# Two more PSUM banks for a first batch, its key load in two, and the next batch's keys ahead of a weight load

## Chip, cores, metric

One core of one Trainium2 chip. The metric is device time in microseconds (us), the median of several runs. Before: 419.73 us (3 runs, 419.38 to 420.42). The profile's span, from the first to the last instruction, is some 2 us shorter than the run that it was taken from.

## The reference

```python
# attention: 8 batches, 16 query heads, 4 key/value heads, 384 tokens, head size 64
k, v  = np.repeat(k, 4, axis=1), np.repeat(v, 4, axis=1)
attn  = softmax(q @ k.T / 8)
x     = (attn @ v) -> tokens x 1024          # 3072 x 1024
h     = np.maximum(x @ w_in, 0.0)            # w_in 1024 x 2048
out   = h * h @ w_out                        # w_out 2048 x 1024
```

The batches flow through one core: attention of batch b+1 is woven between the feed-forward matmuls of batch b. Only batch 0 has no feed-forward work beside it, so its start is the loose end of the kernel.

## The kernel before, where the change touches it

The kernel is recorded by a small scheduler in Python at build time. It keeps a table of assumed costs, and by it decides in which order each engine gets its work. On the chip each engine then runs its list in that order and waits on semaphores. A wrong assumed cost makes no wrong result, but it makes an engine wait in front of something that is not there yet.

First loads of batch 0 (keys and two pairs of query heads), on the queues of SyncE and ScalarE:

```python
keys("sync", 0, 1)          # key group 0, 96 KB
queries("scalar", 0)        # 192 KB
queries("sync", 1)          # 192 KB
keys("scalar", 1, HKV)      # key groups 1 to 3 in one load, 288 KB
```

All other loads are issued by GpSimd, in this order, with copies of keys (`dup_k`) and values (`aug_v`) between them. A copy that waits for its data holds up every load behind it:

```python
load_q(0, 4, 8)             # queries of group 1: "the first query load"
...
load_v(0); load_q(0, 8, 12, 0.6); load_q(0, 12, 16, 0.6)
dup_k(0, 1, 2)
load_w_in(0)
dup_k(0, 2, 3)
load_k(1)
dup_k(0, 3, 4)
aug_v(0, "gpsimd")
load_q(1, 0, 8); load_q(1, 8, 16)
load_w_in(1)
load_v(1)
dup_k(1)
for i in range(2, 6): load_w_in(i)
```

Which PSUM banks transposes and head pairs (the products with the values) may use while batch 0 still has scores to compute; scores have banks 0 to 3:

```python
LOW, MID, HIGH = tuple(range(6)), (4, 5), (6, 7)
...
spare = MID if first else tuple(i for i in LOW if i not in held)
```

w_in comes in eight pieces of 512 KB. Four tiles of the first feed-forward ("lanes", 32 matmuls of 128 rows) need pieces 0 and 1. The first "quad" of four tiles follows (64-row matmuls); its first 16 matmuls need the third piece, and its 17th needs the fourth.

The softmax here doesn't subtract the row's maximum and nothing guards it: scores larger than these inputs give would overflow.

## Time and profile before

| | before |
|---|---|
| time, median (range) | 419.73 us (419.38 to 420.42) |
| span of the profiled run | 418.2 us |
| TensorE busy | 413.4 us, 99% |
| first query load lands | 6.86 us |
| third exponential starts | 7.27 us |
| lanes end | 28.66 us |
| fourth piece of w_in lands | 30.66 us |

Times of landing are those at which the last of a load's 16 semaphore increments came, read from the trace. "Lanes end" is the start of the last lane matmul plus the 0.16 us from one such matmul to the next; the profile models the end of that matmul another 0.16 us later. Besides the lines that the prediction shows, two views of before are needed. The list of loads issued from 1 to 6 us (what it moves, issuing queue, KB, us from issue to landing):

```profile
q_st<-in_q_dram POOLq DMA_DIRECT2D x3, 192.0 KB, 5.5
k_f<-in_k_dram ACTq DMA_DIRECT2D x1, 288.0 KB, 4.0
```

The three key groups land 4.0 us after issue. The second view is the timeline of GpSimd (start, length, engine, line, operation; in brackets an idle time before it and what ended it):

```profile
6.67 0.52 POOL L270 CAST k_dup<-k_f 128x384 bf16<-128x384 f32 x1
7.12 0.76 POOL L209 DMA_DIRECT2D k_st<-in_k_dram  x1
...
9.10 1.76 POOL L241 DMA_DIRECT2D q_st<-in_q_dram  x2
10.84 0.89 POOL L252 DMA_DIRECT2D w_in_sb<-in_moe_w_in_dram  x1
...
13.68 1.47 POOL L270 COPY k_dup<-k_st 128x1536 bf16<-128x1536 bf16 x1 [1.20 <-DMA k_st<-in_k_dram]
```

GpSimd issues both query loads of batch 1 and the second piece of w_in before it waits for anything. Its one wait of 1.20 us, at 12.5, comes when much is under way.

### The profile page before, as it was taken

The page shows a single profiled execution, that of the slowest core. Times are in us where ns is not written, and L with a number is a line of the kernel's source. Part 1 is how long each engine was busy: PE and PEld are TensorE (multiplying, and loading weights), DVE is VectorE, ACT ScalarE, POOL GpSimd, SP SyncE. Part 2 cuts the span into 40 slices and gives each one's busy share as a digit, 9 for nine tenths or more (in the row PEclk, how much of TensorE's full clock was granted, in tenths as well). Part 3 has the DMA queues.
Part 4 walks back from the last instruction along what each step waited for, and adds up shares of the span by engine and source line. Part 5 has one row for each costly group of instructions (what it writes and reads, how often), then busy time and mean ns, then how long its engine had stood idle before and what let it go on. Part 6 is the DMA issues. An engine that isn't in the chain of part 4 may idle for free.

```text
span 418.2 us, 9601 instructions
## 1 busy us (share of the span) xinstructions
PE 413.4 (99%) x4308; PEld 236.2 (56%) x4331; DVE 198.6 (47%) x434; ACT 159.0 (38%) x181; POOL 48.0 (11%) x63
## 2 busy tenths in 40 slices
PE   9999999999999999999999999999999999999997
PEld 6666754557446574455645565456744557445544
DVE  3664751357413782156811666125841458324312
ACT  6948610495009610284104840069000870004300
POOL 8680000323030000200020000000000000000000
PEclk9999999999999999999999999999999999999999
DMA  9999999999996019900499005710052001420012
GB/s 179 190 190 200 206 188 170 260 190 120 187 186 101 2 39 201 209 7 2 61 211 183 2 2 107 183 52 2 3 125 77 27 2 20 122 79 10 0 74 78
DMA packets 96921, 44.40 MB, mean 106 GB/s; under 512 B 77296, under 2 KB 90864, under 8 KB 96880
## 3 DMA queue, kind: packets, MB, share of 16 engines
q0 software_dynamic: 36544, 17.44, 32.5%
q1 hardware_dynamic: 59664, 25.86, 27.7%
q8 instruction: 34, 0.56, 0.5%
q10 hardware_dynamic: 672, 0.49, 0.4%
q14 instruction: 7, 0.06, 0.0%
HBM read 35.65 MB, written 12.58 MB: 115 GB/s over the span
## 4 chain that ended last, share of the span: by engine, by line
PE 97%; ACT 2%; issue 0%; DVE 0%
PE ps L524 39%; PE ps L462 34%; PE ps L367 8%; PE ps L341 7%; PE ps L425 6%; ACT expT L351 2%; PE ps L588 1%; PE ps L400 0%; PE ps L298 0%; PE ps L315 0%; DVE y_sb L533 0%
## 5 line engine op out<-in xcount | busy, mean ns | idle before, releaser
L351 ACT ACTIVATE expT<-ps 128x1024 bf16<-128x1024 f32 (+1 forms) x146 | 136.0, 1022 | 133.4 <-PE ps L341 133.4
L524 PE MATMUL ps<-w_out_sb,h2T 128*128 128x512 bf16 (+2 forms) x761 | 165.7, 375 | 1.2
L462 PE MATMUL ps<-xT,w_in_sb 64*128 64x384 bf16 x1728 | 160.3, 323 | 0.0
L524 PEld LDWEIGHTS ps<-w_out_sb,h2T 128*128 128x128 bf16 x784 | 75.2, 98 | 86.6
L462 PEld LDWEIGHTS ps<-xT,w_in_sb 64*128 64x128 bf16 x1728 | 83.1, 94 | 57.8 <-DVE hr L475 2.1
L475 DVE TENSOR_SCALAR hr<-ps 128x384 f32<-128x384 f32 x108 | 55.2, 553 | 79.0 <-PE ps L462 79.0
L533 DVE COPY y_sb<-ps 128x512 f32<-128x512 f32 (+2 forms) x49 | 33.4, 681 | 112.3 <-PE ps L524 112.3
L341 PE MATMUL ps<-qT,kT 64*128 64x512 bf16 (+2 forms) x384 | 54.3, 326 | 0.3 <-ACT expT L351 0.3
L482 DVE TENSOR_TENSOR h2T<-hr 128x384 bf16<-128x384 f32 x102 | 50.0, 551 | 0.0
L367 PEld LDWEIGHTS ps<-v_aug,expT 128*128 128x128 bf16 x1152 | 37.0, 97 | 5.7 <-issue 1.1
L367 PE MATMUL ps<-v_aug,expT 128*128 128x65 bf16 x1152 | 39.1, 193 | 0.2 <-issue 0.2
L382 DVE TENSOR_TENSOR o_sb<-ps,rinv 128x384 bf16<-128x384 f32 x64 | 35.7, 558 | 2.2
L425 PE MATMUL ps<-xT,w_in_sb 128*128 128x384 bf16 x160 | 27.7, 326 | 0.0
L435 ACT ACTIVATE h2T<-hr 128x384 bf16<-128x384 f32 x20 | 10.3, 522 | 44.3 <-DVE hr L433 44.3
L341 PEld LDWEIGHTS ps<-qT,kT 64*128 64x128 bf16 x384 | 17.8, 94 | 15.6 <-issue 2.1
L275 POOL COPY v_aug<-v_st 128x768 bf16<-128x768 bf16 x8 | 6.6, 830 | 158.4 <-PE ps L367 99.5
L479 ACT ACTIVATE h2T<-hr 128x384 bf16<-128x384 f32 x6 | 3.1, 523 | 51.7 <-DVE hr L475 51.7
L425 PEld LDWEIGHTS ps<-xT,w_in_sb 128*128 128x128 bf16 x160 | 15.4, 98 | 9.7 <-DVE xT L406 0.2
L433 DVE TENSOR_SCALAR hr<-ps 128x384 f32<-128x384 f32 x20 | 11.0, 557 | 12.1 <-PE ps L425 12.1
L241 POOL DMA_DIRECT2D q_st<-in_q_dram x17 | 14.8, 883 | 0.9 <-POOLq L829 0.8
L376 DVE RECIPROCAL rinv<-ps 128x6 f32<-128x6 f32 x64 | 11.9, 186 | 4.4 <-PE ps L367 4.4
L209 POOL DMA_DIRECT2D k_st<-in_k_dram x7 | 5.3, 755 | 43.6 <-DMA qT<-q_st 43.6
(29 smaller groups left out, 65.2 us busy)
## 6 DMA issues: line engine op xcount, KB each, us to landing
out_dram<-y_sb SPq DMA_DIRECT2D x47, 256.0 KB, 2.6
q_st<-in_q_dram POOLq DMA_DIRECT2D x14, 384.0 KB, 8.2
w_in_sb<-in_moe_w_in_dram POOLq DMA_DIRECT2D x8, 512.0 KB, 14.8
w_out_sb<-in_moe_w_out_dram POOLq DMA_DIRECT2D x4, 1024.0 KB, 27.4
v_st<-in_v_dram POOLq DMA_DIRECT2D x8, 192.0 KB, 9.7
k_st<-in_k_dram POOLq DMA_DIRECT2D x7, 192.0 KB, 4.5
q_st<-in_q_dram POOLq DMA_DIRECT2D x3, 192.0 KB, 5.5
xT<-o_sb SPq DMA_TRANSPOSE x28, 2.8
```

Source lines behind the costliest of these rows:

```text
L241: i = R.add("gpsimd", lambda g: g.dma_start(q_st[st][:, h0:h1, :], q[b, h0:h1].rearrange("h (p j) d -> p h (j d)", j=NJ)), writes=[("q_st" ...
L341: mm = pe.matmul(ps[:, base + x, m * wide:(m + 1) * wide], kT[b % 2][64 * x:64 * x + 64, u, :], q_cols(b, u // NJ, x, c0, c0 + wide))
L351: R.add("scalar", lambda e: e.activation(dst, src, AF.Exp, scale=0.125), reads=keys, writes=[("expT", (b * NU + u) % NEX, t) for u, _, _ i ...
L367: m = pe.matmul(po[:, f - 6 * s2, 0:D + 1], w, v_aug[b % 2][:, g * NJ + j, 0:D + 1], start=(j == 0), stop=(j == NJ - 1))
L376: R.add("vector", lambda e: e.reciprocal(rinv[r].ap().unsqueeze(2), po[:, :, D:D + 1]), reads=[("bank", i)], writes=[("rinv", r)], cost=0.22)
L382: R.add("vector", lambda e: e.tensor_tensor(dst, srcv, rbv, ALU.mult), reads=[("bank", i), ("rinv", r)], writes=[("o_sb", o, s2)], cost=0.48)
L425: m = pe.matmul(bank(i)[:, 0:S], w_in_sb[:, kc, c * 128:(c + 1) * 128], xT[b % NXT][:, kc, :], start=(kc == 0), stop=(kc == NKC - 1))
L462: m = pe.matmul(bank(4 + xs[x])[:, 0:S], w_in_sb[r, kc, c * 128:(c + 1) * 128], xT[b % NXT][r, kc, :], start=(phase < 2 and kc == 0), stop ...
L475: R.add("vector", lambda e, r=r, i=i: e.tensor_scalar_max(hr[r][:, :], bank(4 + i)[:, 0:S], 0.0), reads=[("bank", 4 + i)], writes=[("hr", ...
L482: hr_read[r] = (R.add("vector", lambda e, c=c, r=r: e.tensor_tensor(h2T[:, c, :], hr[r][:, :], hr[r][:, :], ALU.mult), reads=[("hr", r)], ...
L524: m = pe.matmul(bank(i)[:, 0:n], h2T[:, c, i3 * 128:(i3 + 1) * 128], w_out_sb[:, c, c0:c1], start=(c == 0), stop=(c == NFC - 1))
L533: R.add("vector", lambda e: e.tensor_copy(ysl, bank(i)[:, 0:n]), reads=[("bank", i)], writes=[("y", yb)], cost=0.08 + n / 960)
```

## The change

The intent: give TensorE more useful work in batch 0. With four banks instead of two, transposes and head pairs need not wait for their copies; batch 1's keys, loaded ahead of w_in, can be transposed then; and the second key group comes in a load of its own, to be there sooner.

```diff
-        keys("scalar", 1, HKV)
+        keys("scalar", 1, 2)
+        keys("sync", 2, HKV)
@@
     dup_k(0, 1, 2)
+    load_k(1)
+    dup_k(0, 2, 3)
     load_w_in(0)
-    dup_k(0, 2, 3)
-    load_k(1)
     dup_k(0, 3, 4)
     aug_v(0, "gpsimd")
     load_q(1, 0, 8)
+    dup_k(1, 0, 2)
     load_q(1, 8, 16)
+    dup_k(1, 2, 4)
     load_w_in(1)
     load_v(1)
-    dup_k(1)
@@
-        spare = MID if first else tuple(i for i in LOW if i not in held)
+        spare = tuple(i for i in MID + HIGH if i not in held) if first else tuple(i for i in LOW if i not in held)
```

Below, the three parts are called "banks", "split" (of the key load) and "order" (of the loads).

## The prediction

> **What bounds the kernel now.** I read the page's busy shares first, then the chain that ended last in order of time, then the timeline of the first 31 us, then each load's time to landing, because the change touches only the first two batches.
>
> The page, busy shares and chain by engine:
>
> ```profile
> PE 413.4 (99%) x4308; PEld 236.2 (56%) x4331; DVE 198.6 (47%) x434; ACT 159.0 (38%) x181; POOL 48.0 (11%) x63
> ...
> PE 97%; ACT 2%; issue 0%; DVE 0%
> ```
>
> TensorE is nearly the whole chain; 2% of 418.2 us is about 8 us of ScalarE. The chain in order of time says where those 8 us lie:
>
> ```profile
> 0.77 3.04 PE ps L588 x27
> ...
> 5.79 8.08 ACT expT L351 x10
> 13.87 0.05 issue
> 13.92 0.39 PE ps L341 x4
> ...
> 24.72 0.17 PE ps L298 x3
> 24.89 0.34 PE ps L315 x6
> ...
> 28.82 0.76 PE ps L462 x8
> ```
>
> The columns are start, length, what. From 5.79 to 13.87 the ten exponentials of the first batch are the chain, and after 13.92 it is TensorE to the end. The second batch's transposes (lines 298 and 315) lie on it at 24.72: 4 x 0.17 + 2 x 0.34 = 1.36 us. So the change can gain only by putting useful TensorE work into holes before 13.9. The timeline shows the holes (start, length, engine, line):
>
> ```profile
> 6.30 0.53 PE L298 MATMUL ps<-ident,k_dup 128*128 128x128 bf16 x3
> ...
> 6.62 0.34 PE L588 MATMUL ps<-const-bfloat16-1.0 128*128 128x128 bf16 x2
> ...
> 6.89 0.34 PE L341 MATMUL ps<-qT,kT 64*128 64x384 bf16 x2
> ...
> 8.32 0.83 POOL L275 COPY v_aug<-v_st 128x768 bf16<-128x768 bf16 x1
> 8.47 0.35 PE L588 MATMUL ps<-const-bfloat16-1.0 128*128 128x128 bf16 x3
> ...
> 10.92 0.44 PE L367 MATMUL ps<-v_aug,expT 128*128 128x65 bf16 x9
> ...
> 13.32 0.34 PE L400 MATMUL ps<-ident,o_sb 128*128 128x128 bf16 x3
> ```
>
> Line 588 is filler. Holes and filler: 6.62 to 6.89 (0.27), 8.05 to 8.20 (0.15), 8.47 to 8.85 (0.38), about 0.1 before 10.25, and about 0.4 between the transposes of 13.32 and the scores of 13.92. Sum: some 1.3 us. That is the ceiling at this end.
>
> There is a second wall later. Waits of 28 to 31.5 us, and the load that ends the wait (KB, us from issue to landing):
>
> ```profile
> PEld ps L462 <- DMA w_in_sb<-in_moe_w_in_dram: 0.4, 1, 0.4
> ```
>
> ```profile
> w_in_sb<-in_moe_w_in_dram POOLq DMA_DIRECT2D x1, 512.0 KB, 14.7
> ```
>
> That load is the fourth piece of w_in, issued at 15.97: it lands at 30.67, and the timeline has TensorE start on it at 30.71. So at 30.7 the kernel is already loading-bound, for a moment.
>
> **What the Trainium skill says.** "PSUM — Partial Sum Buffer", the four PSUM rules: one matmul output goes to one of 8 banks; "Perfetto Trace Analysis", Optimizing Tensor Performance, says independent groups should rotate through banks so that evacuation overlaps the next matmuls. Here batch 0 had banks 4 and 5 for this, each held for the transpose plus a VectorE copy of 0.36 to 0.56 us; the filler at 6.62 agrees, since keys' and queries' copies still held both banks. "DMA: Bandwidth & Descriptors", Issuing engines are not separate DMA queues: loads from different engines run on the same 16 DMA engines, so another issuer saves issue time only. The trace agrees that the engines are the limit (the page has busy tenths of 9 in the first twelve slices of its DMA row). "TensorEngine Tiling (Array Packing)", Key Properties: a change of tiling mode drains TensorE. Each score group (64-row tiles) shows it: about 0.1 us lost on entering and again on leaving, so 0.2 us around each group is not a hole that banks can fill.
>
> **Part by part.**
> *Keys in two loads.* It takes 288 KB as 96 + 192 KB. Before, the load of 1.23 landed after 4.0 us, at 5.23. But GpSimd issues queries until 5.24 and starts the copy of group 1 at 5.33, so an earlier landing brings at most 0.1 us. Off the path: zero.
>
> *Second batch's keys ahead of w_in.* In landing order the loads are last queries of batch 0 (9.9), w_in piece 0 (5.78 + 6.8 = 12.6), k1 (7.12 + 6.5 = 13.6), first queries of batch 1 (9.10 + 7.7 = 16.8). k1 took 13.6 - 12.6 = 1.0 us of the stream, so k1 comes at about 10.9 and w_in piece 0 at about 13.6; all later loads keep their place. The first matmul on w_in is at 15.40, so the 1.0 us later landing still precedes it. The GpSimd copy of 1.47 us, at 13.68 before, becomes two of 0.75 us at about 10.9 and 12.5. It now holds up the issue of the loads behind it by some 2 us, but those have a backlog (second half of batch 1's queries: landing at 18.8, issue about 11.7), so no landing moves.
>
> *Two more banks.* These open until the feed-forward lanes take banks 6 and 7 at about 15. The queue order is fixed at build time from a table of costs in the kernel, which I use for order alone. By hand I get: query transposes of group 1 before the third score group instead of after it; the first value product near 9 instead of 10.92; keys group 0 of batch 1 near 13; queries group 0 of batch 1 near 15.5; keys group 1 near 18. So 0.17 + 0.34 + 0.17 = 0.68 us of the 1.36 leave the chain at 24.7, and products and output transposes move up a little.
>
> Costs, because TensorE executes in order:
> 1. The query transposes that now stand at 6.62 need the load issued at 1.23, which took 5.6 us: 6.86. They run 6.9 to 7.24, and the third score group moves from 6.89 to about 7.34. Third exponential: from 7.27 to about 7.7. Cost to the exponential chain 0.44 us.
> 2. The first value product stands ahead of the sixth score group and needs the value copy (8.32 + 0.83 = 9.15). It delays that group to about 9.66, the exponential to 10.03 instead of 9.38: chain late by 0.65 to 0.7.
> 3. The queries of batch 1 land at 16.8; TensorE would reach their transposes at about 16.1: a wait of some 0.7 us that was not there, with no other work behind it that may overtake.
>
> The lanes' end: in queue order about 0.5 us less work lies ahead of it (0.68 off the end, little else, minus the work displaced). Against this stand about 0.5 us of lag from steps 1 and 2 and 0.7 from step 3: 0.7 later than 28.75, i.e. near 29.5. The following 1.3 us of feed-forward and two score groups then carry it past 30.7, so the wait of 0.15 us for w_in (in excess of the matmul before it) vanishes: net about +0.55. Without step 3 the lanes end where they did: 0. After that TensorE is bound by its own work with fixed order, and a shift is carried to the end undiminished.
>
> **Rivals.**
> (a) *The gain arrives.* If none of the three waits occurs, the lanes end 0.5 to 1.0 us earlier. For: four banks, 1.36 us of transposes. Against: the wall at 30.67, since w_in's fourth piece keeps its landing. Then only the wait moves; at best one more score group (0.22 us) is done before it. Time: 419.4 to 419.7.
> (b) *The extra work only changes places with filler.* Lag of steps 1 and 2 equals the 0.5 us gained: 419.7.
> (c) *The wait for batch 1's queries is real.* 419.7 + 0.55 = 420.3, perhaps 420.6 if the loss of filler keeps the clock low for longer around 6.6. For: one straggler sets the landing at 16.8: of this load's 16 increments the trace has fifteen by 15.6 and the last at 16.8.
> (d) *GpSimd stalls the loads.* Would need a gap in the DMA stream; with loads landing 7 to 15 us after issue I give it 5%, worth up to 1 us.
> A gain of 8 us is impossible, as holes total 1.3; a loss of 8 would need a new stall in the steady batches, which the change doesn't touch.
>
> **Range and chances.** I weigh (c) 0.5, (b) 0.3, (a) 0.2: 0.5 x 420.3 + 0.3 x 419.7 + 0.2 x 419.5 = 420.0. A change that someone kept leans to the good side, so 419.9. The runs of before spread from 419.38 to 420.42, so the range is 419.0 to 420.9. Within 2%: 0.98; 0.01 on either side.
>
> **What would show it.** Right: the filler at 6.62 gone, third exponential at 7.6 to 7.8; first value product at 9.2 to 9.3; the copy of k1 begins at 10.9 or so; TensorE waiting for the queries of batch 1 until 16.8; no more than three transposes groups left at 24 to 26; w_in's fourth piece landing at 30.6 to 30.7 as before. Wrong: if that piece lands half a microsecond or more away from 30.67, if the exponentials keep their old times, or if batch 1's query transposes are not placed before 17. Then (a) or a cause not listed decides.

## The result, and the profile after

| | before | after |
|---|---|---|
| time, median (range) | 419.69 us (419.38 to 420.42), 6 runs | 422.25 us (420.80 to 423.11), 6 runs |
| span of the profiled run | 418.2 us | 420.0 us |
| first query load lands | 6.86 us | 7.89 us |
| third exponential starts | 7.27 us | 8.76 us |
| first piece of w_in lands | 12.62 us | 15.90 us |
| lanes end | 28.66 us | 30.89 us |
| fourth piece of w_in lands | 30.66 us | 32.59 us |

The ratio is 1.0058, with a 95% interval of 1.0037 to 1.0078: within 2%, but slower, and outside the range predicted. A ratio here is the mean time of one kernel's fast runs over that of the other's of the same rounds, so not quite the ratio of the medians quoted. The two profiled runs lie nearer to each other than the medians do: that of before (420.30, a run of its own) is 0.6 us above its median, that of after (421.84) 0.4 us under its median. So their times differ by 1.5 us and their spans by 1.8, where the medians differ by 2.6.

The page of after, its span, the busy times and the chain by engine:

```profile
span 420.0 us, 9602 instructions
...
PE 413.9 (99%) x4308; PEld 237.6 (57%) x4331; DVE 198.9 (47%) x434; ACT 159.2 (38%) x181; POOL 48.0 (11%) x64
...
PE 97%; DMA 2%; issue 0%; DVE 0%; POOLq 0%
```

In place of ScalarE's 2% the chain now has 2% of a DMA. Which one, the chain in order of time says (start, length, what):

```profile
1.23 6.66 DMA q_st<-in_q_dram
7.94 0.51 PE ps L316 x6
...
27.40 0.17 PE ps L299 x3
27.57 0.34 PE ps L316 x6
27.90 0.34 PE ps L299 x6
28.24 2.81 PE ps L426 x17
31.05 0.54 PE ps L342 x4
```

It is the first query load, and TensorE waits for it until 7.94. Of batch 1's transposes 0.17 + 0.34 + 0.34 = 0.85 us are left at 27.40, so 0.51 of the 1.36 us of before are gone from here, as intended; yet the last run of lane matmuls starts at 28.24 and not at 26.06. The timeline of after, 5 to 17 us:

```profile
7.58 0.51 POOL L271 CAST k_dup<-k_f 128x384 bf16<-128x384 f32 x1 [1.15 <-DMA k_f<-in_k_dram]
...
7.94 0.51 PE L316 MATMUL ps<-ident,q_st 128*128 128x128 bf16 x6 [1.60 <-DMA q_st<-in_q_dram]
8.04 0.90 POOL L253 DMA_DIRECT2D w_in_sb<-in_moe_w_in_dram  x1
...
8.76 2.31 ACT L352 ACTIVATE expT<-ps 128x768 bf16<-128x768 f32 x3 [1.49 <-PE ps L342]
...
10.14 0.88 POOL L242 DMA_DIRECT2D q_st<-in_q_dram  x1
...
12.09 0.83 POOL L271 COPY k_dup<-k_st 128x768 bf16<-128x768 bf16 x1 [1.07 <-DMA k_st<-in_k_dram]
...
12.85 0.87 POOL L242 DMA_DIRECT2D q_st<-in_q_dram  x1
```

Three waits are new. TensorE waits 1.60 us for the queries and ScalarE 1.49 us for the scores behind them. GpSimd waits 1.15 us for the keys of the new load and 1.07 us for batch 1's keys, and issues the second query load of batch 1 at 12.85 (before: at 9.98). How the loads fared is seen in the list of loads issued from 1 to 6 us, in after:

```profile
q_st<-in_q_dram POOLq DMA_DIRECT2D x3, 192.0 KB, 6.5
...
k_f<-in_k_dram SPq DMA_DIRECT2D x1, 192.0 KB, 5.9
...
k_f<-in_k_dram ACTq DMA_DIRECT2D x1, 96.0 KB, 3.4
```

and in the traffic of 5 to 17 us, first before, then after with its hardware queue (packets, MB, share):

```profile
DMA packets 5526, 2.23 MB, mean 186 GB/s; under 512 B 4464, under 2 KB 5525, under 8 KB 5525
```

```profile
DMA packets 4883, 2.02 MB, mean 168 GB/s; under 512 B 3700, under 2 KB 4883, under 8 KB 4883
...
q1 hardware_dynamic: 175, 0.12, 4.1%
```

The two key groups that now stand third on SyncE's queue need 5.9 us to land, where all three groups took 4.0. After 5 us they still have 175 packets to move (before has no line of such a queue in this stretch), and these share the engines with GpSimd's queries: from 5 to 6 us GpSimd's queue moves 0.10 MB, where it moved 0.18 before. And 0.21 MB less is moved in these 12 us; at 186 GB/s that is 1.1 us of loading. GpSimd's own queue falls back further, from 2.21 to 1.90 MB, as 0.12 of the 2.02 MB are the late keys.

The end of the first feed-forward, TensorE's timeline from 26 us, before and after:

```profile
28.75 0.82 PE L462 MATMUL ps<-xT,w_in_sb 64*128 64x384 bf16 x8
29.47 0.60 PE L341 MATMUL ps<-qT,kT 64*128 64x512 bf16 x4
29.91 1.62 PE L462 MATMUL ps<-xT,w_in_sb 64*128 64x384 bf16 x16
```

```profile
30.98 0.61 PE L342 MATMUL ps<-qT,kT 64*128 64x512 bf16 x4
31.43 2.12 PE L463 MATMUL ps<-xT,w_in_sb 64*128 64x384 bf16 x24
```

In both, the 17th matmul of the quad is inside the last line: at 30.71 before, at 32.73 after. From it to the end before takes 387.5 us and after 387.2. All of the loss is ahead of it.

**Two walls.** That matmul can start only when (a) the fourth piece of w_in has landed, and (b) the lanes are done and TensorE has done the 16 quad matmuls and two score groups between, which takes 1.84 us in after (30.89 to 32.73) and 1.91 in e10 below, a before in which nothing else holds it (28.63 to 30.54). I read both for every kernel that follows. Before: (a) 30.66, (b) 28.66 + 1.91 = 30.57. After: (a) 32.59, (b) 32.73. The change moved both by about 2 us.

What sets the lanes' end in after is again a load. Where banks and order come together (after, e4, e6, e7, e11, e17), TensorE's list has the transposes of batch 1's first queries among the lanes. Before has them at 24.72, long after their load. After has them here:

```profile
18.09 0.49 PE L316 MATMUL ps<-ident,q_st 128*128 128x128 bf16 x6
```

Their load had landed at 17.95. From there on TensorE has no wait over 0.25 us, and the lanes end 12.80 us later. In the traces of e4, e6, e11 and e17 it is 12.78 or 12.79 us, and each of them has a wait of 0.26 to 0.77 us for this load; in e7 it is 12.64, in the second trace of after 12.95. So both walls of after are late loads.

### The profile page after: what moved, and what is told of

Read it like the earlier page. It is cut to its first block, busy times and chain, and to the rows that moved or that the text cites. A ratio compares the mean times of both kernels' runs of the same rounds, so it can differ in the third digit from the quotient of the medians.

```text
span 420.0 us, 9602 instructions
## 1 busy us (share of the span) xinstructions
PE 413.9 (99%) x4308; PEld 237.6 (57%) x4331; DVE 198.9 (47%) x434; ACT 159.2 (38%) x181; POOL 48.0 (11%) x64
## 3 DMA queue, kind: packets, MB, share of 16 engines
q1 hardware_dynamic: 59936, 26.06, 27.7%
## 4 chain that ended last, share of the span: by engine, by line
PE 97%; DMA 2%; issue 0%; DVE 0%; POOLq 0%
PE ps L525 39%; PE ps L463 33%; PE ps L368 9%; PE ps L342 8%; PE ps L426 6%; DMA q_st<-in_q_dram 2%; PE ps L316 1%; PE ps L401 0%; PE ps L299 0%; PE ps L590 0%; DVE y_sb L534 0%; POOLq L831 0%
## 5 line engine op out<-in xcount | busy, mean ns | idle before, releaser
L463 PEld LDWEIGHTS ps<-xT,w_in_sb 64*128 64x128 bf16 x1728 | 84.0, 94 | 56.5 <-DVE hr L476 2.1
```

Source lines behind the costliest of these rows:

```text
L463: m = pe.matmul(bank(4 + xs[x])[:, 0:S], w_in_sb[r, kc, c * 128:(c + 1) * 128], xT[b % NXT][r, kc, :], start=(phase < 2 and kc == 0), stop ...
```

## The experiments

My theory after the first comparison: the split alone delays the first queries and all loads behind them. Rivals: the order makes GpSimd wait and so delays w_in; the banks make TensorE, which is in order, stand in front of things not there yet; or the clock that falls after the wait costs the time.

They were run in this order: e2, e4, e5, e7; then e1, e3, e6, e8; then e10, e11, e12, e16; then e17, e18. All results are in one table. "Traced" is the time of the one run that was profiled, and the columns after it are read from its trace, in us. "Start of quad's 17th" is the matmul of the two walls, "rest" is from there to the end of the span. MB is what was moved from 5 to 17 us.

| kernel | median, ratio to before [95%] | traced | first queries land | MB | lanes end | 4th piece lands | quad's 17th | rest |
|---|---|---|---|---|---|---|---|---|
| before | 419.69 | 420.30 | 6.86 | 2.23 | 28.66 | 30.66 | 30.71 | 387.5 |
| after (all three) | 422.25, 1.0058 [1.0037, 1.0078] | 421.84 | 7.89 | 2.02 | 30.89 | 32.59 | 32.73 | 387.2 |
| e1 banks | 420.64, 1.0022 [1.0009, 1.0035] | 420.76 | 6.37 | 2.23 | 29.23 | 30.37 | 31.14 | 387.7 |
| e2 split | 420.61, 1.0021 [1.0004, 1.0037] | 422.15 | 8.27 | 2.22 | 30.87 | 31.50 | 32.77 | 387.5 |
| e3 order | 420.65, 1.0020 [1.0006, 1.0034] | 419.31 | 6.48 | 2.24 | 28.34 | 30.12 | 30.25 | 387.2 |
| e4 banks, order | 421.17, 1.0029 [1.0016, 1.0042] | 421.75 | 6.41 | 2.08 | 30.28 | 31.79 | 32.12 | 387.5 |
| e5 split, order | 421.12, 1.0036 [1.0018, 1.0054] | 422.12 | 8.21 | 1.92 | 29.84 | 32.84 | 32.89 | 387.2 |
| e18 banks, split | 421.19, 1.0034 [1.0019, 1.0048] | 422.54 | 7.84 | 2.21 | 31.14 | 31.42 | 33.04 | 387.6 |
| e6 after, split on one queue | 421.58, 1.0039 [1.0026, 1.0053] | 421.85 | 7.62 | 2.12 | 31.04 | 32.46 | 32.88 | 387.1 |
| e7 after, queries assumed later | 421.21, 1.0034 [1.0015, 1.0052] | 422.14 | 7.86 | 1.98 | 31.00 | 32.97 | 33.11 | 387.2 |
| e8 banks, queries assumed later | 420.77, 1.0024 [1.0012, 1.0036] | 421.11 | 6.67 | 2.26 | 29.38 | 30.40 | 31.28 | 387.8 |
| e10 before, w_in earlier | 419.98, 1.0010 [0.9997, 1.0023] | 419.98 | 6.59 | 2.27 | 28.63 | 26.41 | 30.54 | 387.5 |
| e11 after, w_in earlier | 421.46, 1.0044 [1.0032, 1.0056] | 421.85 | 6.51 | 2.14 | 30.79 | 27.63 | 32.62 | 387.2 |
| e12 split, order, w_in earlier | 421.61, 1.0048 [1.0036, 1.0060] | 421.99 | 8.26 | 2.02 | 29.90 | 28.95 | 31.81 | 388.4 |
| e16 split, small part last | 421.05, 1.0038 [1.0017, 1.0059] | 420.82 | 7.14 | 2.08 | 29.74 | 31.23 | 31.65 | 387.2 |
| e17 after, filler in the wait | 422.53, 1.0070 [1.0056, 1.0085] | 421.97 | 8.24 | 2.00 | 30.72 | 32.49 | 32.63 | 387.3 |

A caution on the traces: the walls belong to the traced run and not to the median. The traced runs of e2 and e18 were over a microsecond above the median of their kernel, that of e3 over a microsecond under it. Differences of half a microsecond between two traces may be chance; patterns over several are what I use.

### e1_banks: the banks alone

```diff
-        spare = MID if first else tuple(i for i in LOW if i not in held)
+        spare = tuple(i for i in MID + HIGH if i not in held) if first else tuple(i for i in LOW if i not in held)
```

> The kernel before with the four banks alone; all loads as before. Two-wall theory (what the runs so far say: the time is the later of the landing of w_in's fourth piece and the end of the first feed-forward lanes plus 1.8 us, and a constant 387.3 us follows): the fourth piece lands at 30.4 to 30.9 as before, the lanes end 0.3 us sooner to 0.7 us later than 28.7, the time is 419.4 to 420.2. If the banks themselves cost (value products early, clock falling back), the lanes end after 29.5 and the time is 420.3 or more.

Measured: 420.64, ratio 1.0022: the time of the second expectation, with a lanes' end that the first allowed. No landing that matters came later (the first piece of w_in at 12.72, the fourth at 30.37), but the lanes end 0.57 us later and wall (b) is what counts. The cause is in the timeline of this run:

```profile
7.88 0.35 PE L588 MATMUL ps<-const-bfloat16-1.0 128*128 128x128 bf16 x3
...
8.43 0.35 PE L588 MATMUL ps<-const-bfloat16-1.0 128*128 128x128 bf16 x3
9.31 0.45 PE L367 MATMUL ps<-v_aug,expT 128*128 128x65 bf16 x9 [0.54 <-POOL v_aug L275]
```

The first value product now stands ahead of a score group, at 9.31 as predicted, and waits 0.54 us for the copy of the values; ScalarE then waits 0.57 us for the score group behind it. The filler (line 588) is still there: from 5.2 us on TensorE runs six filler matmuls in this kernel and in after, just as many as before. The banks did not fill holes; they moved them.

### e2_split: the split alone

```diff
-        keys("scalar", 1, HKV)
+        keys("scalar", 1, 2)
+        keys("sync", 2, HKV)
```

> The kernel before with the keys' load split alone (group 1 on ScalarE's queue, groups 2 and 3 as third load of SyncE's queue); banks and order of loads as before. Loading theory: the second keys' load is still moving when GpSimd's first query load starts, the two share the engines, the queries land at 7.6 to 8.0 instead of 6.86, the fourth piece of w_in lands a microsecond or more after 30.67, and the kernel is 1 to 2 us slower (420.7 to 421.7) although no bank and no GpSimd order changed. Order theory (the loss comes of the TensorE order that four banks allow, or of GpSimd waiting for the second batch's keys): within 0.3 us of before.

Measured: 420.61, a shade under what was expected; ratio 1.0021. The first queries land at 8.27 instead of 6.86 and the fourth piece of w_in at 31.50. So a part that I had put down as free costs as much as the banks. The traced run is the only one of the six whose granted clock was under 1.000 (0.996); the other five took 420.19 to 420.82. Under e17 this is taken up.

### e3_order and e3_look2: the order alone

```diff
     dup_k(0, 1, 2)
-    load_w_in(0)
-    dup_k(0, 2, 3)
     load_k(1)
+    dup_k(0, 2, 3)
+    load_w_in(0)
@@
     load_q(1, 0, 8)
+    dup_k(1, 0, 2)
     load_q(1, 8, 16)
+    dup_k(1, 2, 4)
@@
-    dup_k(1)
```

> The kernel before with the second batch's keys ahead of w_in and its copy in two parts; banks and keys' load as before. Two-wall theory: TensorE's order hardly changes, so the lanes end within 0.5 us of 28.7; whatever comes, comes by w_in's fourth piece. If it lands near 30.7 as the blind prediction held (no landing moves), 419.5 to 420.1; if it lands near 31.8 as in the run with banks and order together, 420.6 to 421.2.

> A second trace of the order of loads alone. If its usual run (420.7) is slower by a later landing of w_in's fourth piece, this trace has it at 31 or later and first use there; if TensorE's lanes are what varies, they end after 28.9.

Measured: 420.65 (419.31 to 421.26), ratio 1.0020; the second look was a single run of 420.28, its state unknown. The traces have the keys of batch 1 at 10.63 and 11.05, as the prediction worked out, and the lanes at 28.34 and 28.68, no later than before. The fourth piece lands at 30.12 in one and at 31.05 in the other. In the second TensorE waits 0.34 us for it, the sign that was asked for. That spread is enough to hold the median's 0.9 us, but the traces are of runs quicker than the median, so what costs the order alone its 0.2% is not shown.

### e4_no_split and e5_no_banks: after, with one part undone

```diff
# e4_no_split, against after
-        keys("scalar", 1, 2)
-        keys("sync", 2, HKV)
+        keys("scalar", 1, HKV)
# e5_no_banks, against after
-        spare = tuple(i for i in MID + HIGH if i not in held) if first else tuple(i for i in LOW if i not in held)
+        spare = MID if first else tuple(i for i in LOW if i not in held)
```

> The changed kernel with the keys in one load again; banks and order of loads stay changed. Loading theory: the first query load lands at 6.8 to 7.0, TensorE waits for it 0.2 to 0.4 us instead of 1.7, its clock does not fall back, the fourth piece of w_in lands at 30.4 to 31.0, and the time is that of the blind prediction, 419.4 to 420.4. Order theory: nothing of this helps, 421.5 to 422.5.

> The changed kernel with banks 4 and 5 alone again; split and order of loads stay. Loading theory: the queries still land near 7.9 and w_in's fourth piece near 32.5, so that most of the loss stays, through the later wall of w_in: 421.2 to 422.3. Order theory: the loss is gone, 419.4 to 420.2.

e4 is a miss: 421.17, between the two expectations (420.4 at most, or 421.5 at least). Its queries land at 6.41, so the delay by the split is gone; yet a new wait appears on TensorE's timeline:

```profile
14.01 0.34 PE L400 MATMUL ps<-ident,o_sb 128*128 128x128 bf16 x3
15.45 0.48 PE L425 MATMUL ps<-xT,w_in_sb 128*128 128x384 bf16 x2 [1.10 <-DMA w_in_sb<-in_moe_w_in_dram]
```

The banks bring the first lane matmul forward (14.24 in e1, 15.40 before); the order moves the first piece of w_in back: issued at 7.0 instead of 5.8, and landing at 15.31. Half of its 16 increments are in by 13.3 and the last comes two microseconds later; why, stays open. So the theory of the split alone is out: each two of the parts cost about 0.3%.

e5 is 0.1 us under the range of the loading theory (421.12, expected 421.2 to 422.3) and far from the other. Its trace, of a run a microsecond above the median, shows wall (a) bare. Lanes end at 29.84, and TensorE's timeline has

```profile
31.10 0.81 PE L463 MATMUL ps<-xT,w_in_sb 64*128 64x384 bf16 x8
32.89 0.82 PE L463 MATMUL ps<-xT,w_in_sb 64*128 64x384 bf16 x8 [0.98 <-DMA w_in_sb<-in_moe_w_in_dram]
```

With split and order together, 1.92 MB are moved from 5 to 17 us, the least of all, and the fourth piece is the latest but one. In this kernel GpSimd waits 1.60 us for the split keys, then 0.94 us for batch 1's, and issues the second query load of batch 1 at 13.18.

### e6_split_one_queue: both key loads on one queue

```diff
# against after
         keys("scalar", 1, 2)
-        keys("sync", 2, HKV)
+        keys("scalar", 2, HKV)
```

> The changed kernel with both keys' loads on ScalarE's queue, one behind the other, instead of the second on SyncE's. If it is the place of the second load (third on SyncE's queue, issued at 1.66) that lets it run into GpSimd's first query load, then here, still third on a queue and issued at about 1.7, it does the same: queries at 7.6 to 8.3, time 421.5 to 422.8. If SyncE's queue is what is slow, the queries land near 6.8 and the time is that of the run without a split, 421.1.

Measured: 421.58, the first queries at 7.62. The queue on which the last keys come makes no difference that I can resolve; that they come as a third load does.

### e7_late_turn and e8_banks_late_turn: a truer table

Both tell the build-time table that the first queries come later, so that their transposes are not put ahead of the third scores.

```diff
# e7 against after (1.6), e8 against e1_banks (0.6)
-    load_q(0, 4, 8)
+    load_q(0, 4, 8, 1.6)
```

> The changed kernel with 1.6 us added to the first query load in the table of costs that orders the queues, so that its transposes stand behind the third and fourth score group. Same loads, same banks. If the wait of TensorE at 6.2 is itself the loss, the time falls by 1 to 2 us, to 420.3 to 421.2. If the later landing of w_in (fourth piece near 32.5) is a wall of its own, the wait at 6.2 shrinks to under 0.5 us and the time stays within 0.7 us of the changed kernel's 422.25.

> The kernel before with four banks and 0.6 us added to the first query load in the ordering table, so that its transposes stand behind the third and fourth score group. TensorE should then not wait for the queries at all. Two-wall theory: the lanes may end sooner than 28.7, but the fourth piece of w_in still lands at 30.4 to 30.9, so the time is 419.3 to 420.0, no more than 0.4 us better than before.

e7: the third exponential is back at 7.43 and still the lanes end at 31.00 and the fourth piece lands at 32.97. The order of TensorE in this place is not what holds the lanes; the queries themselves, and the loads behind them, are late; and the value product, now one place ahead, waits 1.51 us for the copy of the values. Its median is 1.0 us under after's, with both walls no lower in its trace. But that trace is of its second slowest run (422.14) and after's of one of the quicker ones, so what its quicker runs did is not traced. e8 is a miss (at most 420.0 expected) and brings nothing over e1 (420.77 against 420.64): the wait for the value copy just grows from 0.54 to 0.73 us.

### e10_early_w_in, e11_after_early_w_in, e12_no_banks_early_w_in: wall (a) taken down

The second and third pieces of w_in go ahead of the second query load of batch 1, and the fourth ahead of its values.

```diff
# e11, against after (e10: the same on before; e12: on e5_no_banks)
     dup_k(1, 0, 2)
-    load_q(1, 8, 16)
-    dup_k(1, 2, 4)
     load_w_in(1)
+    load_w_in(2)
+    dup_k(1, 2, 4)
+    load_q(1, 8, 16)
+    load_w_in(3)
     load_v(1)
-    for i in range(2, 6):
+    for i in range(4, 6):
```

> The kernel before with the third and fourth piece of w_in ahead in GpSimd's queue (third before, fourth right after the second half of the second batch's queries; the values after it). The wall of w_in's fourth piece falls from 30.66 to 27 to 29; the lanes stay. Two-wall theory: the time is then set by the end of the lanes (28.7) plus 1.8, i.e. 30.5 in place of 30.7, so 0.0 to 0.4 us better than before. A loss of over 0.5 us would mean that the later queries or values became a wall of their own.

> The changed kernel with the same early third and fourth piece of w_in. Two-wall theory: in the changed kernel both walls stand at the same height (fourth piece 32.59, lanes' end 30.89 plus 1.84), so taking one away brings next to nothing: 421.3 to 422.6 against 422.25. If w_in alone were the cause, the time falls by 1.5 us or more, to 420.7 or less.

> The changed kernel with banks 4 and 5 alone and early w_in. In its twin without early w_in the lanes ended at 29.84 and the fourth piece landed at 32.84, so there w_in alone is the wall. Two-wall theory: the first matmul on the fourth piece comes at 31.4 to 32.0 instead of 32.9, and the time is 0.5 to 1.3 us under that twin's (421.12 median, 1.0036 of before).

In all three the fourth piece lands some four to five microseconds sooner, and none gets clearly quicker for it (e11 has 1.0044 where after has 1.0058, with intervals that overlap). In e10 and e11 the lanes (28.63, 30.79) hold the quad's 17th matmul where it was: 30.54 and 32.62. That shows wall (b) to be as high as wall (a) in before and in after. e12 is a miss. The wait of 0.98 us of e5 is gone from TensorE's timeline,

```profile
31.16 1.46 PE L463 MATMUL ps<-xT,w_in_sb 64*128 64x384 bf16 x16
32.46 0.38 PE L342 MATMUL ps<-qT,kT 64*128 64x256 bf16 x4
```

and the 17th matmul comes 1.1 us sooner, at 31.81, but the rest takes 388.4 us instead of 387.2: TensorE waits again, about 0.45 us for the sixth piece of w_in (landed at 38.63, used from 38.77) and 0.53 us at 81.34 for a later batch's queries. I had expected a gain of 0.5 to 1.3 us over e5 and got none. Loads further on in the stream have become the wall.

### e16_small_last and e18_banks_split: how big, and the missing pair

```diff
# e16, against before
-        keys("scalar", 1, HKV)
+        keys("scalar", 2, HKV)
+        keys("sync", 1, 2)
```

e18 is before with the banks and the split of the change.

> The kernel before with the keys' load split the other way round: groups 2 and 3 (192 KB) second on ScalarE's queue, group 1 (96 KB) third on SyncE's. Loading theory, as a dose: what counts is how many bytes the late third load shares with GpSimd's first queries; half the bytes of the change's third load give half its delay, queries at 7.0 to 7.5 (6.4 to 6.9 without a split in five traces, 7.6 to 8.3 with 192 KB last). If any third load costs the same whatever its size, 7.6 to 8.3.

> The kernel before with four banks and the split, order of loads as before: the last of the eight combinations. The parts alone gave 1.0022, 1.0021 and 1.0020. If they add, this pair gives 1.0040 (421.4). If the split's late queries make the banks' early transposes wait as in the changed kernel (about 1.7 us), more than the sum: 1.0045 to 1.0060 (421.6 to 422.2).

With 96 KB in the third load instead of 192 KB the first queries land at 7.14, between the 6.37 to 6.90 of the seven traces without a split (before, e1, e3 twice, e4, e8, e10) and the 7.62 to 8.27 of nine of the ten with 192 KB. That agrees with the expectation that the size of the late load sets the delay, but it is a single trace (and e11, 6.51, is an exception that I cannot explain). The time is no better than with the split of e2 (421.05, with a wide interval). In its trace group 1, which is needed first, comes last: its copy waits 1.78 us, and TensorE 1.22 us for that copy. e18 measured 1.0034, a little under the 1.0040 that I had expected at least.

### e17_filler_in_wait: the clock

After TensorE's wait, the granted clock of after falls. The table of busy time by stretch, after, for 9 to 12 us (start and end, length, then PE, PEld, DVE, ACT, POOL busy with counts, then the granted clock, the DMA share and GB/s):

```profile
9.00:10.00 1.00, 1.00 (x7) 0.36 (x7) 0.38 (x2) 1.00 (x2) 1.00 (x2) 0.52 1.59 190
10.00:11.00 1.00, 1.00 (x14) 0.83 (x12) 0.00 (x0) 1.00 (x2) 1.00 (x2) 0.50 1.24 135
11.00:12.00 1.00, 1.00 (x10) 0.60 (x8) 0.00 (x0) 0.44 (x2) 0.02 (x1) 0.50 1.29 171
```

From 9 to 12 us TensorE is at half clock; before has 1.00 in each of these. If that is what costs the time, filler in the wait should win it back.

```diff
# against after; warm_up takes a bank
             b, g, w = turn_q.pop(0)
+            if (b, g, w) == (0, 1, "q"):
+                warm_up(24, 0.0, 5)
```

> The changed kernel with 24 filler matmuls (1.34 us at full clock) ahead of the query transposes that wait, in a bank that is free. If the falling clock is a cost of its own, no run shows a granted clock under 1.0, score groups keep their short spacing from 8.4 to 12.3, the lanes end 0.5 to 1.0 us sooner than 30.9; the time then falls only if w_in's fourth piece does not hold it: 421.2 to 422.3. If the clock hardly matters, the lanes end within 0.3 us of 30.9 and the time stays at 421.8 to 422.7.

The filler did what it was meant to, on TensorE's timeline and in the core's clock:

```profile
6.10 1.57 PE L590 MATMUL ps<-const-bfloat16-1.0 128*128 128x128 bf16 x24
8.29 0.51 PE L316 MATMUL ps<-ident,q_st 128*128 128x128 bf16 x6 [0.62 <-DMA q_st<-in_q_dram]
```

```profile
core 0: 419.9 us, clock 1.000
```

All four runs had a clock of 1.0, and the time is 422.53, not lower than after's. The lanes end 0.17 us sooner and the fourth piece lands at 32.49: the walls are where they were. TensorE did gain by the full clock: from the query transposes to the first lane matmul it took 7.39 us (8.29 to 15.68) instead of after's 8.27 (7.94 to 16.21). But then it has to wait for batch 1's queries, which after reached just as they landed:

```profile
17.94 0.49 PE L316 MATMUL ps<-ident,q_st 128*128 128x128 bf16 x6 [0.48 <-DMA q_st<-in_q_dram]
```

So in after the fallen clock is not the cost: that load holds the lanes anyway. Where the load does not stand in the way, the clock does cost. In e2 and e5 TensorE has the same list up to the lanes, and waits equally long for the first queries. From 9 to 13 us e2 had a granted clock of 0.63, 0.50, 0.50 and 0.66, e5 of 1.00. The transposes after the wait and the first lane matmul, first in e2, then in e5:

```profile
8.40 0.49 PE L316 MATMUL ps<-ident,q_st 128*128 128x128 bf16 x6 [1.42 <-DMA q_st<-in_q_dram]
...
17.60 0.49 PE L426 MATMUL ps<-xT,w_in_sb 128*128 128x384 bf16 x2
```

```profile
8.34 0.50 PE L316 MATMUL ps<-ident,q_st 128*128 128x128 bf16 x6 [1.41 <-DMA q_st<-in_q_dram]
...
16.58 0.49 PE L426 MATMUL ps<-xT,w_in_sb 128*128 128x384 bf16 x2
```

That is 9.20 against 8.24 us, a loss of 0.96 in e2, with no wait of its TensorE over 0.25 us in between. The times of runs agree with a cost: in each of e2, e5, e7, e11, e16 and e18 the runs with a granted clock of 0.992 or 0.996 (8 of 33) are slower than all of that kernel's runs at 1.000. In e16 it is three of six: 421.28 to 422.84, against 419.86 to 420.82. In after, where it is four of six, the order is not so clean (421.78 to 423.11, against 420.80 and 422.65); no run of before whose clock is on record has it. Such runs raise the means and some medians in the table. How much of it is the clock, and how much the wait before it, the times alone do not separate.

### after_look2: the changed kernel once more

> A second trace of the changed kernel. First query load lands at 7.6 to 8.3 (six of seven traces with the 192 KB load last did so), TensorE waits for it over 1 us, both walls stand at 32 or later.

A single run of 422.16, its state unknown: first queries at 7.79, lanes 30.84, fourth piece 32.81, 2.08 MB. The two walls of after are not the chance of one trace.

### What the set says together

Fourth piece of w_in, by parts: 30.37 to 30.66 with neither split nor order; 31.23 to 31.50 with a split alone or with banks (e2, e16, e18); 30.12 to 31.79 with the order (e3 twice, e4); 32.46 to 32.97 in all six traces with both and the loads otherwise as in after (after twice, e5, e6, e7, e17). Each delays the stream a little and the two together by 2 us. The lanes end at 28.34 and 28.68 with the order alone, 29.23 with the banks, 30.28 with both, 29.84 with split and order, and 30.89 with all. The traces of the split without the order scatter (29.74 in e16, 30.87 and 31.14 in e2 and e18, whose clock fell), so I do not divide this wall among the parts. In time the parts cost 0.22, 0.21 and 0.20% alone, 0.29 to 0.36% in pairs, 0.58% together, with intervals of 0.13 to 0.2% to either side: about additive within these, and no single part to blame. No kernel beat before; e10 equals it.

## Why the prediction was wrong, point by point

- *Keys in two loads: "Off the path: zero".* This step failed first. I asked only whether an earlier group 1 would help, and not what the third load on a queue does to the loads beside it. It held the first queries to 7.62 to 8.27 us in nine traces of ten (6.86 before), and GpSimd's copy of group 2, hence the issue of w_in, to 8.04 (6.99 in e4, which has the order and the banks but not the split). The Trainium skill's "DMA: Bandwidth & Descriptors", in "Queues, rings and completion order", says that each DMA engine takes turns between the queues that have packets for it. The 175 packets on SyncE's queue after 5 us agree with that; I had cited another section of the page and drawn from it only that issue time is saved.
- *"So no landing moves."* This step failed with it, and carried the most. It rested on loads having a backlog. In after GpSimd waits 1.15 and 1.07 us in copies that now stand ahead of loads; from 10 to 11 us 135 GB/s are moved, where it was 197 before; 0.21 MB less is moved by 17 us; the first piece of w_in lands at 15.90, not at 13.6, the first queries of batch 1 at 17.95, not at 16.8, and the fourth piece at 32.59, not at 30.6 to 30.7. With the order alone the step came nearer (the first piece at 13.87 and 14.46, the fourth at 30.12 and 31.05 in the two traces). It is my rival (d), which I gave 5% and at most 1 us; it was about 2 us at wall (a), with the split's share in it. The prediction named this landing as the sign of its failing, and so it was.
- *Step 1, 0.44 us to the exponential chain.* Right in kind, a third of its true size: the third exponential starts at 8.76 instead of 7.27, 1.49 us later, as the queries land a microsecond later than the 6.86 that I took. In e1 and e4, where they land early, the third exponential starts at 7.23 and 7.27, so there the step costs nothing at all.
- *Step 2, the value product at 9.2 to 9.3 behind the value copy.* Right where the split is absent: 9.31 in e1, 9.22 in e4. In after everything there is a microsecond later, and it starts at 10.45.
- *Step 3, a wait for batch 1's queries.* Right as a mechanism; the term that was mis-sized is the landing. They are transposed at 18.09, when they have just landed (17.95, not 16.8), and the lanes end 12.80 us later. With the 16.8 that I used, the same 12.80 would give 29.6, next to the 29.5 that I predicted. So wall (b) too stands where it does because landings moved.
- *Half a microsecond less work ahead of the lanes' end.* Too much. By the kernel's own table the order of after brings the lanes' end 0.27 us forward and that of the banks alone puts it off by 0.09; the number of filler matmuls did not change. Of the 1.36 us of transposes 0.51 left the late place (predicted: 0.68; keys group 1 was not placed near 18 but stayed at 27.40), and they were paid for early.
- *What held.* TensorE's order up to the queries of batch 1 came out as worked out by hand. After the quad's 17th matmul the rest takes 387.1 to 387.8 us in every trace but e12's, so a shift is carried to the end undiminished. Rival (c) had the direction, and its load is the one that holds wall (b). And the wall of w_in was seen; that it moves was not.

The two walls also explain why no single repair brings the time of before back: taking down (a) leaves (b) at the same height (e11), undoing the banks leaves (a) (e5), undoing the split leaves a late first piece of w_in (e4), and undoing the order leaves the late first queries, in its trace with a fallen clock (e18).

Still open: why single loads straggle by one or two microseconds at their last increment (w_in's first piece in e4); the 0.2% of the order alone; why a pause of 1.4 us is followed by a fall of the clock in e2 and not in e5; and how much of each median is due to runs whose clock fell.

## What to carry to other kernels

A load that is split so as to come sooner is also one more load that comes later, and it takes its bytes from whatever is in flight then: look up what that is before calling it free. Where one engine both copies and issues loads, count the waits of every copy placed ahead of an issue. And where a trace shows two things ready at the same moment, as here w_in's landing and the work in front of it within 0.2 us, a gain on one brings nothing, while a loss on either is paid in full.

## What the Trainium skill lacked or had wrong

- "DMA: Bandwidth & Descriptors": it says that loads of different engines interleave, and that spreading them only saves issue time. It gives no size for what it can cost. Here 192 KB as a third hardware-queue load put off the landing of a 192 KB load of GpSimd: between 6.37 and 6.90 us in seven traces without it, between 7.62 and 8.27 in nine of ten with it; with 96 KB it was 7.14 (one trace).
- "TensorE: Matmul & The Clock Gate", Part 1, the HAM clock gate: it has the clock fall back after at least one idle window of about 3.4 us. In after a pause of 1.60 us between matmuls was followed by a granted clock of 0.52 to 0.50 from 9 to 12 us, and with the pause mostly filled (e17) the clock stayed at 1.000. A pause of 1.42 us was followed by 0.63 to 0.50 in e2, one of 1.41 us by 1.00 in e5. The page also calls the window free-running, which would fit such chance; the threshold itself is not measured here, but a pause of under half of it was enough.
